# Talking-heads attention and Fourier mixing: score copies placed right behind the scores in five steps of a batch

## The chip, the core and the metric

The kernel runs on one core of a Trainium2 chip. The metric is the device time of one execution in microseconds (us), lower is better; the number compared is the median over runs. The engines of the core that matter here: TensorE (PE) does matmuls and transposes into PSUM, VectorE (DVE) and ScalarE (ACT) read PSUM and write SBUF, GpSimd (POOL) works on SBUF alone and starts many of the transfers, SyncE (SP) starts the others.

## The reference

Two blocks, in float32, for 8 batches of 448 positions and 12 heads of 64:

```python
scores = scale * np.matmul(q, k.transpose(0, 1, 3, 2))
scores = np.einsum('bhij,hg->bgij', scores, w_pre)        # heads are mixed
attn = np.exp(scores - np.max(scores, axis=-1, keepdims=True))
attn = attn / (np.sum(attn, axis=-1, keepdims=True) + 1e-09)
attn = np.einsum('bhij,hg->bgij', attn, w_post)           # and mixed again
attn_out = np.matmul(attn, v)
# x: (8, 448, 768), the heads side by side
mixed = np.real(np.fft.fft(np.fft.fft(x, axis=1), axis=2))
u = x + mixed
un = (u - mean(u)) / sqrt(var(u) + 1e-06)
out = u + np.maximum(un @ w_ch1, 0.0) @ w_ch2             # 768 -> 3072 -> 768
```

## The kernel before

The program has two stages. The mixing stage (`mix_phase`) makes u, the feed-forward stage (`ffn_phase`) makes the output. Only the mixing stage is touched.

**How the mixing stage is tiled.** The rows of a batch are cut into 8 blocks, and the blocks into 23 steps (`GS`); 8 batches make 184 steps (`TOT`). A step handles 10 positions with all 12 heads: two tiles of 5 positions, x = 0 and 1. Below, s is the number of a step and m = s mod 23 its place in the batch.

**What happens to a step T**, in the order of its data:

- *Scores* (`emit_qk`, matmuls at L628): q times k for a block and a pair of heads, into two PSUM tiles called "ms". Two copies on ACT (`copy`, L489) bring them to SBUF as "Sb". A block needs three such calls.
- *Gather* (`emit_gather`, L645): four transfers that SP starts turn rows of Sb into "Kr", where the heads of one position lie on partitions. Issued five steps ahead.
- *First head mix* (`emit_premix`, L656), two steps ahead: PE writes "mx", two PSUM tiles, one for each x, one buffer each.
- *Maximum* (`emit_max`, L663, DVE) of each mx, negated, as "nmx".
- *Exponential* (`emit_exp`, L670, ACT) of each mx with nmx as bias, into "PP", with the row sum into "den"; reading the sum out is an instruction of its own behind each.
- *Scaling* (`emit_scale`): DVE adds a constant to the sums (L677) and takes the reciprocal (L678), POOL multiplies PP (L680).
- *Second head mix* (`emit_postmix`, L690), in the step itself: PE writes "po". DVE transposes it into "Pv" (`emit_turn`, L703).
- *Values* (`emit_av`, L720): Pv times v for a group of two blocks, into two "ms" tiles; copies on ACT into "XT".

Beside these run "full" jobs: transposes of the next batch's q and k (`emit_xpose`, L601, copied half by ACT and half by DVE, all at L489), transposes of XT (`emit_x`, L764), and the Fourier products (`emit_z`, L829; `emit_s2`, L845, whose results DVE adds into X at L856 and L858). Each takes one or two "ms" tiles. DVE also does one conversion of the feed-forward weights in each step ("conv", `wts.deal(1)`, lines 250 to 310), for the double-precision inputs.

**The four "ms" buffers.** The pool `pms` has 4 buffers in turn. A job's matmuls are emitted at once; the copy that empties its tiles is put into the list `pend` and emitted by `flush()`. A fifth tile waits on the copy out of the first. `take` empties the list before each "full" job, and `room(2)` before scores and values when it would hold more than four.

**What sets the order.** The stage runs under `manual_schedule`: PE, DVE, ACT and POOL execute in the order in which the loop emits. One step is emitted in one of two orders, for even and for odd s:

```python
ORDERS = tuple(o.split() for o in (
    "pre post flush AV max0 exp0 "
    "QK max1 exp1 turn scale conv full gather",
    "pre post flush max0 max1 QK exp0 "
    "AV turn exp1 scale conv gather full flush"))
```

"pre", "max", "exp" and "scale" are of step s + 2, "post" and "turn" of step s, "gather" of step s + 5. The words "QK", "AV" and "full" take those jobs whose due time has come. A batch begins at an even s or an odd one in turn, so a given m has the even order in half of the batches and the odd order in the others.

**The five places.** In m = 0, 2, 5, 13 and 15 two more jobs that use "ms" tiles follow the scores, or take their place beside a second set of scores. m = 0: scores, L845, L764. m = 2: two scores, L845. m = 5 and 13: scores, L764, L601. m = 15: scores, L601 twice. In the first, second and last batch some of these jobs are missing: steps 23, 166 and 174 have one of the two, step 25 has two scores alone, step 176 has no scores.

Of the kernel before, what the change touches and what calls it, by code (L numbers as in the profile page):

```python
# [45 lines left out]
GS = BLOCK_AT[-1]  # L46
# [47 lines left out]
AT_QK = ((0, 2, 1), (0, 1, 2), (0, 1, 2), (1, 2, 2),  # L94
         (0, 1, 2), (0, 1, 2), (0, 1, 2), (0, 1, 2))
AT_AV = ((1, 2, 4), (0, 1, 3), (1, 3, 5), (1, 3, 4))
AT_X = ((13, 0), (23, 1), (28, 3), (29, 2))
AT_Z = (39, 40, 40, 42)
AT_S = ((42, 44), (46, 48))
# [351 lines left out]
def mix_phase(ctx, tc, rest, ident, q, k, v, w_pre, w_post, u_scr, u_rev, wts, lead):  # L451
# [39 lines left out]
    def flush():  # L491
        while pend:
            pend.pop(0)[1]()

    def room(n):
        if sum(e[0] for e in pend) + n > 4:
            flush()
# [138 lines left out]
    def emit_gather(T):  # L636

        Kr = pkr.tile([P, 2, S], F32, name="Kr", tag="Kr")
        n, j = at_step[T]
        Sb, rs = blocks[n]["Sb"], blocks[n]["rs"]  # L640
        row = _row(Sb)
        for z in range(2):
            for x in range(2):
                p0 = 64 - R * rs + 4 * j + 2 * z + x
                (nc.gpsimd if x and T < 3 else nc.sync).dma_start(  # L645
                    out=Kr[64 * x:64 * x + KR, z, :],
                    in_=_ap(Sb, p0 * row, [[rs * row, 2 * R], [S, 6], [1, S]]))
        steps[T]["Kr"] = Kr
# [25 lines left out]
    def emit_scale(T):  # L674
        PP, den = steps[T]["PP"], steps[T]["den"]
        rcp = psm.tile([P, 2], F32, name="rcp", tag="rcp")
        nc.vector.tensor_reduce(rcp[:, :], den[:, :, :], axis=AX.X, op=ALU.add)  # L677
        nc.vector.reciprocal(out=rcp[:, :], in_=rcp[:, :])  # L678
        for x in range(2):
            nc.gpsimd.tensor_scalar(PP[:, x, :], PP[:, x, :], rcp[:, x:x + 1], 1.0,  # L680
                                    op0=ALU.mult, op1=ALU.mult)
# [203 lines left out]
    def due(kind, at, fn):  # L885
        fill[kind].append((at, len(fill[kind]), fn))
# [4 lines left out]
    for b in range(B):  # L891
# [31 lines left out]
        for n in range(NG):  # L923
            for pr in range(3):
                due("AV", f + GROUP_AT[n + 1] + AT_AV[n][pr],
                    lambda a=b * NG + n, pr=pr: (emit_av(a, pr), None))
            at, gi = AT_X[n]
            if b == B - 1 and n > 1:
# [27 lines left out]
    def take(kind, s):  # L956
        large = 0
        while fill[kind] and fill[kind][0][0] <= s:
            fn = fill[kind].pop(0)[2]
            if kind == "none":  # L960
                large += bool(fn())
            elif kind == "full":
                flush()
                pend.extend((1, e, None) for e in fn())
            else:
                room(2)
                evs, n = fn()
                pend.extend((1, e, n) for e in evs)
        return large

    s = int(min(v_[0][0] for v_ in fill.values()))
    ET = mybir.EngineType
    with tc.manual_schedule(engines={ET.PE, ET.DVE, ET.Activation, ET.Pool}):
        while s <= TOT - GS + AT_X[-1][0]:
            old = len(later)
            n = take("none", s)
            ahead, now = 0 <= s + LM < TOT, 0 <= s < TOT
            for op in ORDERS[s % 2]:
                if op == "flush":
                    flush()  # L980
                elif op in fill:
                    take(op, s)
                elif op == "conv":
                    if s >= 4:
                        wts.deal(1)
                elif op == "gather":
                    if 0 <= s + LG < TOT:
                        if any(e[2] is not None and e[2] <= at_step[s + LG][0] for e in pend):
                            flush()
                        emit_gather(s + LG)  # L990
                elif op == "scale":
                    if ahead:
                        emit_scale(s + LM)
                    for _ in range(old if s < TOT + 5 else 0):
                        later.pop(0)()

                    if s < TOT - 3:
                        for _ in range(min(len(folds), 1 if n and s > 3 else 2)):
                            folds.pop(0)()
                elif op in ("post", "turn"):  # L1000
                    if now:
                        (emit_postmix if op == "post" else emit_turn)(s)
                elif ahead:
                    (emit_premix if op == "pre" else emit_max if op[0] == "m"
                     else emit_exp)(s + LM, *map(int, op[3:]))
            s += 1
        flush()
        wts.deal(1000)
# [484 lines left out]
@with_exitstack  # L1493
def kernel(
    ctx: ExitStack,
    tc: tile.TileContext,
    q: bass.AP,
    k: bass.AP,
    v: bass.AP,
    w_pre: bass.AP,  # L1500
    w_post: bass.AP,
    moe_w_ch1: bass.AP,
    moe_w_ch2: bass.AP,
    out: bass.AP,
):
    nc = tc.nc
    base = ctx.enter_context(tc.tile_pool(name="base", bufs=1))
    scr = ctx.enter_context(
        tc.tile_pool(name="scr", bufs=1, space=bass.MemoryType.DRAM))
    ident = base.tile([P, P], F32, name="ident")  # L1510
    make_identity(nc, ident[:, :])
    u_scr = [scr.tile([S + 1, DM], F32, name=f"u_{b}") for b in range(B)]
    u_rev = [scr.tile([S + 1, DM], F32, name=f"v_{b}") for b in range(B)]
    ub_scr = [scr.tile([7, P, NK, TB // 2], F32, name=f"ub_{t}") for t in range(NTB)]
    wts = _Weights(nc, moe_w_ch1, moe_w_ch2, scr)
    lead = _Lead(ctx, tc, ident, u_scr, u_rev)
    rest = ExitStack()
    fold_rest, parts = mix_phase(tc, rest, ident, q, k, v, w_pre, w_post, u_scr, u_rev,
                                 wts, lead)
    ffn_phase(tc, rest, ident, u_scr, u_rev, wts, ub_scr,  # L1520
              out.rearrange("b s d -> (b s) d"), fold_rest, parts,
              lead)
# [31 lines left out]
```

## Time and profile before

| quantity | value |
|---|---|
| median of 3 runs | 2296.27 us (2294.4 to 2301.48) |
| profiled execution | 2299.42 us, of which the span from the first to the last instruction is 2297.6 us |
| granted TensorE clock, mean | 0.998 |
| mixing stage, steps 0 to 181 | 36.5 to 776.2 us of the span |
| PE busy in the stretch from 100 to 215 us | 112.7 of 115.0 us |
| one score copy (L489, Sb) | 0.54 us, 378 of them on ACT |
| one exponential (L670) | 0.63 us, 368 |
| one maximum (L663) | 0.62 us, 368 |
| one scaling (L680) | 0.65 us, 368 |

Durations and waits are taken from one profiled execution, by the hardware profiler. In its lines, an engine's name is followed by the line of the program, the operation, and out<-in by the program's names of tiles. In a timeline the first two numbers are the start, in us from the beginning of the span, and the duration; "x16" merges 16 instructions that follow each other; "[0.23 <-ACT Sb L489]" says that the engine was idle for 0.23 us before and that a copy on ACT ended this. A line of the table of waits gives the total, how often, and the longest. A matmul's end is modelled, so a PE that is shown busy can still be slowed down. Where two exponentials are shown with their read-outs (ACTIVATION_READ_ACCUMULATOR), the end of the pair is the end of the second read-out.

### The profile page before, as it was taken

The numbers are of one execution on the slowest core, as the hardware profiler recorded it, in microseconds if no ns is written. First come the engines' busy times: TensorE is split into PE (matmuls) and PEld (weight loads), VectorE is DVE, ScalarE is ACT, GpSimd is POOL, SyncE is SP. The second block draws the span as 40 slices with busy tenths as digits, with TensorE's granted clock in tenths as the row PEclk, the third lists the DMA queues.
The fourth block names the chain that finished last, engine by engine and source line by source line (L and its number), as shares of the span: only waits on it lengthen the run. The fifth ranks groups of instructions, "written<-read, shape, count | busy, mean of one in ns | idle before, by whom it ended". The sixth has DMA issues, their size and how long they took to land.

```text
span 2297.6 us, 60793 instructions
## 1 busy us (share of the span) xinstructions
PE 2249.2 (98%) x22894; PEld 1740.7 (76%) x22894; DVE 1711.2 (74%) x3640; ACT 1167.1 (51%) x3330; POOL 1292.1 (56%) x1805
## 2 busy tenths in 40 slices
PE   7999999999999999999999999999999999999998
PEld 3455555555554677777899999999999899999998
DVE  5778787888877757776877787778778777765545
ACT  4676767767676533231445445444444445434434
POOL 7677878879768541221555555546555645454334
PEclk9999999999999999999999999999999999999999
DMA  7566565666756475649677887788787987795664
GB/s 185 168 178 181 168 192 171 190 179 181 202 151 190 143 265 182 230 162 327 191 181 180 252 214 184 212 195 242 204 197 184 277 188 174 191 257 121 143 146 76
DMA packets 228063, 439.45 MB, mean 191 GB/s; under 512 B 35964, under 2 KB 149558, under 8 KB 227772
## 3 DMA queue, kind: packets, MB, share of 16 engines
q1 hardware_dynamic: 156620, 301.52, 38.2%
q0 software_dynamic: 68864, 133.00, 30.4%
q8 instruction: 183, 3.00, 0.6%
q10 hardware_dynamic: 2288, 1.05, 0.2%
q14 instruction: 108, 0.88, 0.1%
HBM read 213.16 MB, written 143.16 MB: 155 GB/s over the span
## 4 chain that ended last, share of the span: by engine, by line
PE 87%; DVE 5%; DMA 3%; ACT 2%; issue 1%; POOL 1%; SPq 1%; ACTq 0%; DVEq 0%; POOLq 0%
PE psP L1213 18%; PE psP L1335 14%; PE psR L1213 9%; PE psR L1335 7%; PE mx L656 6%; PE ms L720 6%; PE ms L628 5%; PE po L690 5%; PE psQ L1213 4%; PE psQ L1335 3%; PE psP L1290 3%; PE ms L845 2%; PE ms L601 2%; DMA Kr<-Sb 1%; PE psR L1290 1%
## 5 line engine op out<-in xcount | busy, mean ns | idle before, releaser
L1369 POOL DMA_DIRECT2D out_dram<-od x172 | 209.1, 1276 | 261.7 <-DVE od L1357 175.3
L680 POOL TENSOR_SCALAR PP<-PP,rcp 128x448 f32<-128x448 f32 x368 | 234.6, 647 | 170.2 <-DVE rcp L678 123.8
L670 ACT ACTIVATE PP<-mx,nmx 128x448 f32<-128x448 f32 x368 | 230.2, 631 | 165.2 <-DVE nmx L663 157.2
L663 DVE TENSOR_REDUCE nmx<-mx 128x1 f32<-128x448 f32 x368 | 212.5, 618 | 101.2 <-PE mx L656 99.1
L1176 POOL TENSOR_TENSOR hq<-h 128x128 f32<-128x128 f32 (+1 forms) x210 | 130.0, 619 | 255.9 <-ACT h L1235 122.3
L1363 ACT COPY od<-psP 128x192 f32<-128x192 f32 x488 | 156.1, 320 | 172.0 <-PE psP L1335 170.6
L1366 DVE TENSOR_TENSOR od<-od 128x768 f32<-128x768 f32 x210 | 201.3, 972 | 52.7 <-ACT od L1363 52.3
L703 DVE STREAM_TRANSPOSE Pv<-po 128x896 f32<-128x896 f32 x184 | 203.7, 1107 | 2.9 <-PE po L690 2.1
L489 ACT COPY Sb<-ms 124x448 f32<-124x448 f32 (+1 forms) x378 | 181.7, 540 | 46.0 <-PE ms L628 19.2
L656 PE MATMUL mx<-Kr,kw 60*32 60x448 f32 x2944 | 192.2, 549 | 4.3 <-ACT PP L670 2.3
L628 PE MATMUL ms<-kT,qT 64*32 64x448 f32 (+1 forms) x3072 | 191.6, 545 | 3.9 <-ACT qT L489 2.8
L720 PEld LDWEIGHTS ms<-Pv,vv 64*64 64x64 f32 x5376 | 138.1, 132 | 73.7 <-issue 48.8
L690 PE MATMUL po<-PP,kw 60*32 60x448 f32 x2944 | 184.0, 537 | 1.2 <-POOL PP L680 1.1
L1213 PE MATMUL psP<-qs,w1t 128*128 128x256 f32 x744 | 179.2, 380 | 2.4 <-DVE h L1234 1.5
L1213 PE MATMUL psP<-ks,w1t 128*128 128x256 f32 x744 | 179.3, 380 | 0.4 <-DVE h L1234 0.3
L720 PE MATMUL ms<-Pv,vv 64*64 64x120 f32 (+1 forms) x5376 | 160.8, 263 | 3.6 <-ACT Sb L489 2.2
L254 POOL TENSOR_SCALAR wst<-wst 128x256 f32<-128x256 f32 (+1 forms) x76 | 118.6, 1569 | 67.2 <-ACT wst L265 66.9
L1213 PEld LDWEIGHTS psP<-qs,w1t 128*128 128x128 f32 x744 | 139.5, 190 | 19.4 <-DVE h L1234 1.9
L1213 PEld LDWEIGHTS psP<-ks,w1t 128*128 128x128 f32 x744 | 139.5, 190 | 17.2 <-DVE h L1234 0.7
L1213 PE MATMUL psP<-ub,w1t 128*128 128x256 f32 x528 | 127.2, 379 | 1.1 <-DVE h L1234 1.1
L1234 DVE TENSOR_TENSOR h<-h,psP 128x512 f32<-128x512 f32 x42 | 28.8, 686 | 127.9 <-PE psP L1213 112.3
L1335 PE MATMUL psP<-w2t,hq 128*128 128x192 f32 x490 | 122.5, 332 | 1.2 <-DVE od L1357 1.2
(199 smaller groups left out, 5301.6 us busy)
## 6 DMA issues: line engine op xcount, KB each, us to landing
Kr<-Sb SPq DMA_DIRECT2D x730, 105.0 KB
out_dram<-od POOLq DMA_DIRECT2D x172, 384.0 KB, 6.3
qs<-ub SPq DMA_DIRECT2D x89, 384.0 KB
ks<-ub SPq DMA_DIRECT2D x88, 384.0 KB
ub<-ub SPq DMA_DIRECT2D x79, 384.0 KB
w1t<-w SPq DMA_DIRECT2D x42, 384.0 KB
w2t<-w SPq DMA_DIRECT2D x42, 384.0 KB
raw<-in_moe_w_ch_dram SPq DMA_DIRECT2D x32, 384.0 KB
```

The costliest lines, as they stand in the source:

```text
L628: nc.tensor.matmul(pss[x][o:o + hi - lo, :S], st["qT", xx][64 * x:64 * x + 64, y, lo:hi], st["kT", xx][64 * x:64 * x + 64, y, :], start=Tr ...
L656: nc.tensor.matmul(mx[x][64 * z + o:64 * z + o + 32, :S], kw1[64 * x:64 * x + KR, o:o + 32], Kr[64 * x:64 * x + KR, z, :], start=True, sto ...
L663: nc.vector.tensor_reduce(nmx[:, :], steps[T]["mx"][x][:, :S], axis=AX.X, op=ALU.max, negate=True)
L670: nc.scalar.activation(steps[T]["PP"][:, x, :], steps[T]["mx"][x][:, :S], ACTF.Exp, bias=steps[T]["nmx", x][:, :], accum_out=steps[T]["den ...
L680: nc.gpsimd.tensor_scalar(PP[:, x, :], PP[:, x, :], rcp[:, x:x + 1], 1.0, op0=ALU.mult, op1=ALU.mult)
L690: nc.tensor.matmul(po[o:o + 32, z, :S], kw2[64 * z:64 * z + KR, y, :], PP[64 * z:64 * z + KR, :, c * HS:(c + 1) * HS], start=True, stop=True)
L703: nc.vector.transpose(turned[a]["Pv"][:, j, :].rearrange("p (z s) -> p z s", z=2), steps[T]["po"][:, :, :S])
L720: nc.tensor.matmul(pss[y][64 * x:64 * x + 64, :nu * R], st["v", pr][64 * y:64 * y + 64, x, jb * D:(jb + 1) * D], _ap(Pv, 64 * y * rp + 32 ...
L1213: mm = nc.tensor.matmul(p[:, m, :], w1[i][:, kc, m * P:(m + 1) * P], ub[:, kc, :], start=i in (0, 4, 1)[:3 - seed] and m == kc == 0, stop= ...
L1335: nc.tensor.matmul(ps[j, key][:, :DQ], a, b, start=m in (0, 4), stop=True, skip_group_check=True)
L1366: eng.tensor_tensor(D[j][:, :, :], D[j][:, :, :], D[k][:, :, :], op=ALU.add)
L1369: nc.gpsimd.dma_start(out=acc[t, r, d], in_=D[j][:, :, :], accum_op=ALU.add)
```

## The change

After the word "QK" of a step whose m is in `TWO`, all that stands in `pend` is emitted at once. In a step of the even order the score copies thus come on ACT behind the first exponential and in front of the second; in a step of the odd order they come in front of both. Before, they came behind both, when the next "full" job was taken or at the next "flush". In the other 18 places of a batch nothing changes.

```diff
 AT_AV = ((1, 2, 4), (0, 1, 3), (1, 3, 5), (1, 3, 4))
+TWO = (0, 2, 5, 13, 15)
 AT_X = ((13, 0), (23, 1), (28, 3), (29, 2))
...
                 elif op in fill:
                     take(op, s)
+                    if op == "QK" and s >= 0 and s % GS in TWO:
+                        flush()
                 elif op == "conv":
```

The function that it calls, unchanged:

```python
    def flush():
        while pend:
            pend.pop(0)[1]()
```

## The prediction

> **What bounds the kernel now.** I read the page's first part, then the table of waits, then the timeline engine by engine around the five steps that the change names.
>
> ```profile
> PE 2249.2 (98%) x22894; PEld 1740.7 (76%) x22894; DVE 1711.2 (74%) x3640; ACT 1167.1 (51%) x3330; POOL 1292.1 (56%) x1805
> ```
>
> TensorE (PE) has almost no gap, so the end moves by what PE waits. The waits that the change aims at are those for a copy of scores (Sb, L489), in microseconds, times, longest:
>
> ```profile
> PE ms L601 <- ACT Sb L489: 6.9, 19, 1.2
> PE ms L845 <- ACT Sb L489: 2.7, 6, 0.6
> ```
>
> Together 9.6 us: that is the most there is to gain. Below, m is the step's place in its batch, a step starts at its first L656 matmul, and bare times run from that start. Step 97 (m = 5, odd) on PE:
>
> ```profile
> 434.79 0.96 PE L628 MATMUL ms<-kT,qT 64*32 64x448 f32 x16
> 435.68 0.91 PE L764 MATMUL ms<-ident,XT 128*113 128x128 f32 x6
> 436.82 0.98 PE L601 MATMUL ms<-ident,rawq 128*128 128x128 f32 x7 [0.23 <-ACT Sb L489]
> 437.73 0.98 PE L656 MATMUL mx<-Kr,kw 60*32 60x448 f32 x16
> ...
> 440.99 0.61 PE L656 MATMUL mx<-Kr,kw 60*32 60x448 f32 x8
> ```
>
> L628 (scores) and L764 take the four "ms" buffers; L601 needs the first one back and waits 0.23 us for its copy. Next step at 437.73, the one after at 440.99. ScalarE (ACT) in it:
>
> ```profile
> 435.00 0.63 ACT L670 ACTIVATE PP<-mx,nmx 128x448 f32<-128x448 f32 x1 [0.46 <-DVE nmx L663]
> ...
> 436.14 0.20 ACT L670 ACTIVATION_READ_ACCUMULATOR PP<-mx,nmx 128x1 f32 x1
> 436.24 0.96 ACT L489 COPY Sb<-ms 124x448 f32<-124x448 f32 x2
> ...
> 440.71 0.20 ACT L670 ACTIVATION_READ_ACCUMULATOR PP<-mx,nmx 128x1 f32 x1
> ```
>
> The exponentials run from 435.00 to 436.34, the copies behind them. The next pair ends at 440.91, 0.08 us before the step at 440.99 opens: its L656 overwrites the "mx" buffers that they read. VectorE (DVE):
>
> ```profile
> 436.45 0.16 DVE L677 TENSOR_REDUCE rcp<-den 128x2 f32<-128x4 f32 x1
> 436.64 0.17 DVE L678 RECIPROCAL rcp<-rcp 128x2 f32<-128x2 f32 x1
> 436.72 1.29 DVE L310 TENSOR_TENSOR wst<-wst 128x256 f32<-128x256 f32 x1
> 437.94 1.12 DVE L489 COPY qT<-ms 128x512 f32<-128x512 f32 x1
> 438.89 1.11 DVE L663 TENSOR_REDUCE nmx<-mx 128x1 f32<-128x448 f32 x2
> ```
>
> The sum (L677) needs both exponentials, and behind it DVE is packed up to the next maxima (L663), which the next exponentials need. In step 59, where ACT was late by chance, DVE stood still there:
>
> ```profile
> 276.60 0.16 DVE L677 TENSOR_REDUCE rcp<-den 128x2 f32<-128x4 f32 x1 [0.92 <-ACT PP L670]
> ```
>
> What late exponentials cost PE, step 18 (m = 18) shows:
>
> ```profile
> 103.78 1.20 PE L656 MATMUL mx<-Kr,kw 60*32 60x448 f32 x12
> ...
> 108.43 0.96 PE L656 MATMUL mx<-Kr,kw 60*32 60x448 f32 x16
> ```
>
> Its first half opened when the first exponential was done, 0.56 us before the second one ended at 104.34. The step lasts 4.65 us; the other batches' m = 18 last 4.04 to 4.07. No gap is recorded, yet the lateness of the second exponential is paid in full. So a step opens, in effect, at the end of the previous step's second exponential + 0.06.
>
> **What the Trainium skill says.** "PSUM — Partial Sum Buffer", section "Engine vs sequencer instructions": the queues of ScalarE, VectorE and GpSimd are strict first in, first out, and matmuls keep program order; step 59's line agrees (0.92 us of standing still). "TensorEngine Tiling (Array Packing)", section "PSUM Bottleneck": tiling speeds up the matmuls, not the emptying of PSUM; agreed: 16 score matmuls hold PE 0.89 us in the excerpt (434.79 to 435.68), the two copies ACT 0.96. "Trainium Kernel Development and Optimization", section "Performance Expectations": matmul busy time is a bad metric; agreed by step 18, so I compare the lengths of steps.
>
> **The change part by part.** Nothing is added or removed. On PE the order of instructions is the same row for row, likewise on DVE and POOL. On ACT the score copies of m = 0, 2, 5, 13, 15 move: in even steps in front of the second exponential, in odd steps in front of both. SP's gathers shift by one or two places against a store: nothing, since PE waits 0.8 us in all for Kr in this stage. Prices from the timeline: a pair of copies 0.96 us, starting 0.10 us after the scores end; a pair of exponentials 1.34, one 0.72; the waiting product can start 0.58 after the first copy's start; L677 0.10 after the last exponential. Each follower overlaps by 0.12.
>
> *Odd step (97).* Scores end at 2.46. Copies 2.56 to 3.52 instead of 2.95 to 3.91, so L601 starts at about 3.25 instead of 3.53: +0.28 of gain. The exponentials move from 1.72-3.06 to 3.40-4.74. The next step could open at 4.17 but opens at 4.80, where it opened at 4.45: loss 0.35. Then DVE: L677 at 4.84 instead of 3.17. With c for the weight instruction (1.29 here), the maxima come at 4.84 + c + 1.14 = 7.27 instead of 5.61; the exponentials end 2.05 later, and the step after next opens at 9.38 instead of 7.71: loss 1.67.
>
> *Even step (82, m = 13).* First exponential as before, copies 2.59 to 3.55, second exponential to 4.15 (was 3.08). Next step at 4.21 instead of 4.47: gain 0.26. L677 is 1.06 later; the maxima with c = 0.28 at 5.87 instead of 5.50, the exponentials at 7.92: inside the step's 3.83 (4.21 + 3.83 = 8.04). Gain 0.26 stays.
>
> The same working for all, loss at the start of the second step after, in us:
>
> - m = 5. Odd 51, 97, 143: 1.5, 1.7, 1.5. Even 28, 74, 120: the maxima at 4.25 + c + 1.14, c 0.8 to 1.04; loss 0.56 each. 166 has no third product, and its next step moves from 3.26 to 4.21: 0.95. Sum 7.3.
> - m = 13. Odd 13, 151, 105: 0.35, 0.35, 0.26; 59, where PE had waited 1.0, gains 0.4. Even 82, 128 gain 0.26 each; 36 loses 0.25, 174 (no third product) 0.95. Sum 1.3.
> - m = 15. DVE copies two chunks (1.6 us), and the next scores need the buffer of the first. Odd 15, 61, 107, 153: 1.05, 0.6, 0.8, 0.55. Even 38, 84, 130: 0.3, 0.2, 0.15. Sum 3.6.
> - m = 0. No PE wait to remove. DVE's four L856/L858 (1.95) come behind L677 and free a buffer that the next step's first product needs: odd 69, 115, 161 end them at 7.4, where that product stood at 6.2: 1.2 each; even 92, 138: 6.9 against 6.1, 0.8 each; 46 nothing, PE was late itself. 23: next step 3.85 to 5.4: 1.6. Sum 6.8.
> - m = 2, four copies. Odd 71, 117, 163: exponentials end at 5.60, L677 at 5.70, L856/L858 to 8.4, maxima 8.3 instead of 7.3: 1.1 each. 25 has no third product, next step 3.01 to 5.66: 2.65. Even 48, 94, 140: second exponential to 4.98, 0.64 each. Sum 7.8.
> - Steps 0, 2, 5: PE waits there for transfers as well; bounds -1 and +4, I take 1.5.
>
> POOL's scaling (L680) comes 1.1 to 1.7 later behind L678; median 3.3 us lie between its end and its reader L690, so I take nothing. What is queued behind it on POOL (loads, folds) has steps of room; where POOL is behind (a slack of 0.05 at steps 35, 36, 53, 104, 167, 168) the bounds are -2 (PE's lateness hides its wait) and +3.
>
> Sum: 7.3 + 1.3 + 3.6 + 6.8 + 7.8 + 1.5 = 28.3. Other waits of PE in this stage (L720 2.2, L656 on ACT 2.3, L628 1.1, POOL 1.1, "issue" 1.1, Kr 0.8: 8.6 us) partly vanish under a later PE; I take off a third, 3. Left: +25. The profiled execution took 2299.4 (span 2297.6 + 1.8), so 2324; against the median of the runs, 2296.3, it is 2321.
>
> **Rivals.**
>
> 1. Only the first delay counts: DVE makes good its lateness. Odd 0.35 x 11 + 0.27 x 3 + 0.4 x 3, 23 and 25 4.2, 166 and 174 1.9, minus eight even gains of 0.26: about +10, 2306. For it: DVE is 74% busy overall. Against: in step 97 it has no idle from L663 to the next L663.
> 2. Gains and losses cancel: 2296, if m = 0 and 2 cost nothing and m = 5 half. Against: steps 25, 166, 174 can only lose.
> 3. Faster: buffers come back early and the exponentials' delay is covered. All 9.6 us go: 2287. It decides if L656 can open without the end of both exponentials, or if DVE's work behind L677 has over 1.7 us of room. For it: the waits are there, and step 6's L656 stood 1.4 us behind the exponentials in 97. Against: step 18, and the 0.08 us at 440.99.
>
> That the copies stay where they were is ruled out by ACT's order.
>
> **How the numbers follow.** My forecast 0.66, rival 1 0.16, rival 2 0.08, rival 3 0.10. Under about 0.3% (6.9 us) this measurement can't be told from no change. Faster 0.10, same 0.08, slower 0.82. Forecast's own bounds: 28.3 + 2.5 + 3 = 34 above, 28.3 - 2.5 - 2 - 8.6 = 15 below; down to rival 1 at +10: 2305 to 2330.
>
> **What would show it.** Right: L677 waits for ACT PP in odd steps by about 1.7 us, PE mx L656 <- ACT PP and ms waits for DVE grow, the waits for Sb shrink under 4 us; steps 97 and 98 together last 9.4 us, not 7.7; step 25 lasts 5.7, not 3.0. FFN stage unchanged. Wrong: if step pairs keep their length, or the page's DVE idle does not move to L677.

## The result

The median went from 2296.74 to 2325.63 us, six executions of each on the same chip (2293.8 to 2303.92 and 2320.33 to 2328.85). The medians lie 28.9 us apart; the ratio is 1.0118, 95% interval 1.0105 to 1.013, which is 27.1 us of the time before. The profiled execution took 2326.35 us with a span of 2324.0, at a mean granted clock of 0.996 (before: 0.998).

The mixing stage, steps 0 to 181, took 768.3 us instead of 739.7: 28.6 more. What comes behind it took 1519.1 instead of 1521.4, and that figure lies between 1517.7 and 1521.0 in the other kernels below, so no change of the FFN stage shows. From here on, line numbers are one higher than before (L656 is L657 and so on) because of the new line at the top, and three higher below the loop.

The first part of the page of the kernel after (busy time of each engine, share of the span, instructions):

```profile
PE 2274.3 (98%) x22894; PEld 1758.0 (76%) x22894; DVE 1702.1 (73%) x3640; ACT 1167.5 (50%) x3330; POOL 1291.5 (56%) x1805
```

The same 22894 matmuls are busy for 25.1 us longer, while the idle time of PE grew by 1.3 us only (span minus busy: 48.4 before, 49.7 after). Who looks for the loss among the gaps of PE does not find it. Part 5 of the page (group of instructions | busy us, mean ns of one | idle before it, with what ended it) shows where it lies. Before:

```profile
L656 PE MATMUL mx<-Kr,kw 60*32 60x448 f32 x2944 | 192.2, 549 | 4.3 <-ACT PP L670 2.3
```

And after:

```profile
L657 PE MATMUL mx<-Kr,kw 60*32 60x448 f32 x2944 | 219.3, 551 | 14.7 <-ACT PP L671 9.1
```

One matmul is as long as before (549 and 551 ns), but the group covers 27.1 us more: its sixteen instructions are torn apart, since part of them wait for the second exponential while the others run. The table of waits of the kernel after, PE (us in total, times, longest):

```profile
PE mx L657 <- ACT PP L671: 9.1, 11, 1.9
...
PE ms L629 <- DVE kT L490: 3.9, 7, 0.8
...
PE ms L602 <- ACT Sb L490: 0.5, 1, 0.5
```

The waits for score copies are gone as intended (6.9 to 0.5 at L602, 2.7 to none at L846). And DVE:

```profile
DVE nmx L664 <- PE mx L657: 88.7, 89, 6.0
...
DVE rcp L678 <- ACT PP L671: 73.9, 44, 3.5
```

The sum (L678) now stands still for 73.9 us in all, where the table of before has 14.6 in 16 waits. Here is step 97 again, which starts at 448.84 (start, us, instruction). PE:

```profile
450.35 0.96 PE L629 MATMUL ms<-kT,qT 64*32 64x448 f32 x16
...
451.98 0.98 PE L602 MATMUL ms<-ident,rawq 128*128 128x128 f32 x7
453.04 1.20 PE L657 MATMUL mx<-Kr,kw 60*32 60x448 f32 x12
...
454.06 0.56 PE L657 MATMUL mx<-Kr,kw 60*32 60x448 f32 x4
...
457.11 1.20 PE L657 MATMUL mx<-Kr,kw 60*32 60x448 f32 x12
```

L602 no longer waits. The next step opens in two halves. The line with x12 merges two groups: by the starts of the single matmuls, the eight of L657 for the first tile start from 453.04 on, and the first four for the second tile at 453.66, 0.06 us after the end of the second exponential; the line at 454.06 is the other four of that tile. In the kernel before all sixteen start within 0.44 us. ACT:

```profile
451.40 0.97 ACT L490 COPY Sb<-ms 124x448 f32<-124x448 f32 x2 [1.29 <-PE ms L629]
452.25 0.65 ACT L671 ACTIVATE PP<-mx,nmx 128x448 f32<-128x448 f32 x1
...
456.33 0.63 ACT L671 ACTIVATE PP<-mx,nmx 128x448 f32<-128x448 f32 x1 [1.18 <-DVE nmx L664]
```

ACT stands idle for 1.29 us because it waits for scores; behind that wait two exponentials are queued whose inputs, the maxima, are both there at 451.00, before the scores are. DVE:

```profile
453.71 0.16 DVE L678 TENSOR_REDUCE rcp<-den 128x2 f32<-128x4 f32 x1 [1.69 <-ACT PP L671]
...
453.99 0.78 DVE L311 TENSOR_TENSOR wst<-wst 128x256 f32<-128x256 f32 x1
454.69 1.13 DVE L490 COPY qT<-ms 128x512 f32<-128x512 f32 x1
455.60 1.16 DVE L664 TENSOR_REDUCE nmx<-mx 128x1 f32<-128x448 f32 x2
```

The sum waits 1.69 us; the conversion, the qT copy and the maxima follow it without a gap; and the exponentials of the next step start at 456.33, so late that the step after next is late too.

The growth of the mixing stage by place, counted from each of the five places up to the next one, so that a delay that shows one or two steps later is with its cause (steps 0, 2, 5 apart; differences of two profiled executions, worked out from the starts of the steps):

| place | predicted, us | measured, us | in odd steps | in even steps |
|---|---|---|---|---|
| m = 0 | 6.8 | 3.1 | 23: 1.57; 69, 115, 161: 0.41, 0.26, 0.35 | 46, 92, 138: 0.42, 0.10, 0.01 |
| m = 2 | 7.8 | 11.4 | 25: 4.17; 71, 117, 163: 1.84, 1.57, 1.74 | 48, 94, 140: 0.57, 0.66, 0.85 |
| m = 5 | 7.3 | 2.5 | 51, 97, 143: 0.49, 2.29, 0.91 | 28, 74, 120: 0.10, -0.05, 0.33; 166: -1.61 |
| m = 13 | 1.3 | 1.1 | 13, 59, 105, 151: 0.34, -0.60, 1.41, 0.44 | 36, 82, 128: -0.91, -0.27, -0.27; 174: 0.95 |
| m = 15 | 3.6 | 7.0 | 15, 61, 107, 153: 1.34, 1.22, 1.55, 1.28 | 38, 84, 130, 176: 0.69, -0.14, 0.89, 0.15 |
| steps 0, 2, 5 | 1.5 | 3.5 | 5: -1.04 | 0: 3.02; 2: 1.53 |
| sum | 28.3 | 28.6 | 21.5 | 7.0 |

The sum agrees, its terms do not. Two of the figures are not the place's own, -1.61 at step 166 and a part of 3.02 at step 0; the section on why the prediction was right takes them up. The experiments ask whether the mechanism is right all the same, and which terms were wrong.

### The profile page after: what moved, and what is told of

Read it like the earlier page. It is cut to its first block, busy times and chain, and to the rows that moved or that the text cites. A ratio compares the mean times of both kernels' runs of the same rounds, so it can differ in the third digit from the quotient of the medians.

```text
span 2324.0 us, 60841 instructions
## 1 busy us (share of the span) xinstructions
PE 2274.3 (98%) x22894; PEld 1758.0 (76%) x22894; DVE 1702.1 (73%) x3640; ACT 1167.5 (50%) x3330; POOL 1291.5 (56%) x1805
## 4 chain that ended last, share of the span: by engine, by line
PE 87%; DVE 4%; issue 4%; ACT 2%; POOL 1%; DMA 1%; SPq 0%; DVEq 0%; POOLq 0%; ACTq 0%
PE psP L1216 17%; PE psP L1338 14%; PE psR L1216 9%; PE mx L657 7%; PE psR L1338 7%; PE ms L629 6%; PE ms L721 6%; PE po L691 5%; PE psQ L1216 4%; PE psQ L1338 3%; PE psP L1293 2%; PE ms L846 2%; PE ms L830 1%; ACT PP L671 1%; DMA Kr<-Sb 1%
## 5 line engine op out<-in xcount | busy, mean ns | idle before, releaser
L657 PE MATMUL mx<-Kr,kw 60*32 60x448 f32 x2944 | 219.3, 551 | 14.7 <-ACT PP L671 9.1
L629 PE MATMUL ms<-kT,qT 64*32 64x448 f32 (+1 forms) x3072 | 204.5, 544 | 9.6 <-DVE kT L490 3.9
L691 PE MATMUL po<-PP,kw 60*32 60x448 f32 x2944 | 206.9, 539 | 0.7 <-issue 0.6
L629 PEld LDWEIGHTS ms<-kT,qT 64*32 64x32 f32 (+2 forms) x3072 | 63.9, 105 | 81.6 <-issue 54.7
```

The lines of the kernel that those rows point to most:

```text
L629: nc.tensor.matmul(pss[x][o:o + hi - lo, :S], st["qT", xx][64 * x:64 * x + 64, y, lo:hi], st["kT", xx][64 * x:64 * x + 64, y, :], start=Tr ...
L657: nc.tensor.matmul(mx[x][64 * z + o:64 * z + o + 32, :S], kw1[64 * x:64 * x + KR, o:o + 32], Kr[64 * x:64 * x + KR, z, :], start=True, sto ...
L691: nc.tensor.matmul(po[o:o + 32, z, :S], kw2[64 * z:64 * z + KR, y, :], PP[64 * z:64 * z + KR, :, c * HS:(c + 1) * HS], start=True, stop=True)
```

## The experiments

Where not said otherwise a kernel is the one after with the edit shown. The theory: the late exponentials hold PE by two ways, the first gate (the next step's L657 needs both exponentials done) and the queue of DVE (L678 waits for them, and the next maxima stand behind it).

**1 and 2. Odd steps alone, even steps alone.**

```diff
-                    if op == "QK" and s >= 0 and s % GS in TWO:
+                    if op == "QK" and s >= 0 and s % 2 and s % GS in TWO:
```

> The copies move only in the steps of the odd order, where they pass both exponentials. My theory (late exponentials hold the next first head mix, and the sums behind them hold the vector engine): the step lengths of the changed kernel put 21.6 us on the odd steps, so about 2318 us. Rival (the first wait alone, both orders alike): half of the loss, about 2311.

Measured: 2315.81 against 2297.03 before, ratio 1.0076 [1.0059, 1.0093]. The second kernel has `s % 2 == 0` in place of `s % 2`:

> The copies move only in the steps of the even order, where they pass one exponential. My theory: the step lengths put 7.0 us on the even steps, so about 2304 us, 5 of it in the first batch and m = 2. Rival (both orders alike): about 2311.

Measured: 2310.64, ratio 1.0056 [1.0039, 1.0072]. The odd steps came out 2 us below what was expected. The even ones missed: 6.6 us above the expectation, at the figure of the rival. The two shares add up to 1.32%, where the whole change measured 1.18%; the intervals cover that. A part of the miss is found: in the profile of the even steps the mixing stage is 10.7 us longer, 3.7 more than the 7.0 of the table, and all of these 3.7 lie at steps 166 to 168 (+2.07 here, -1.61 in the kernel after), where step 168 waits for transfers of Kr (8.33 us here, 6.71 before, 4.64 in the kernel after). The rest, some 3 us between this profile and the medians, stays open. What stands: both parities lose, and odd steps more than even ones (2313.9 to 2317.2 us against 2308.7 to 2312.2).

**3 and 4. The queue of DVE taken out.** In the five places the sum and the scaling are emitted at the end of the step, behind DVE's other work of that step, and the copies stay early. On POOL the scaling thereby comes behind the other work of the step, too.

```diff
                 elif op == "scale":
-                    if ahead:
+                    if ahead and not (s >= 0 and s % GS in TWO):
                         emit_scale(s + LM)
...
+            if ahead and s >= 0 and s % GS in TWO:
+                flush()
+                emit_scale(s + LM)
             s += 1
```

> The changed kernel, but in the five steps the sums, reciprocals and scaling of the exponentials are emitted at the end of the step, behind the weight conversion and the copies of the full jobs. My theory: the vector engine no longer stands still, its wait for ACT PP (73.9 us) falls under 40, and what is left is the first wait of the next head mix, the steps 25, 166 and 174 and the first batch: about 2311 us. Rival (the time goes to the first wait alone, or to transfers): stays at 2325.

And the control, the same move in the kernel before, with the copies late as they were there:

> Control: the kernel before with the same later place of sums and scaling in the five steps and the copies where they were. My theory: no engine waits for the sums there, so 2297 within 3 us. If it moves by more, the run sums_late has to be read against this one.

Measured: 2317.7, ratio 1.0083 [1.0066, 1.0099], about halfway between the theory (2311) and the rival (2325); the control 2304.52, ratio 1.0031 [1.0019, 1.0043]. The control was expected at no change and missed: the move itself costs some 7 us, mostly two steps behind m = 2 (steps 50, 96 and 142 are 1.1 us longer each), and the waits of L691 for POOL's scaling become 5.2 us in all (1.1 before). The move did what it was for; the table of waits of the third kernel, DVE:

```profile
DVE rcp L678 <- ACT PP L671: 13.5, 11, 3.8
```

From 73.9 back to 13.5. Step by step, m = 2 in 71, 117, 163 falls to 0.54, 0.67, 0.64 (from 1.6 to 1.8), and m = 15 in 61, 107, 153 to 0.39, 0.57, 0.38 (from 1.2 to 1.6), while step 13, where only the first gate was predicted to act, keeps its 0.34. Steps 25 and 38 lose more than in the kernel after (5.64 and 3.86 us); there the granted clock was 0.50 for 6.8 and 3.4 us in this profile. Taken as it stands, the loss falls from 1.18% to 0.83%. If the move costs the same with and without early copies, the early copies cost 0.52% when the queue of DVE is out, and 1.18% when it is in. Each end has an interval of some 0.15%. That the costs add is not shown, and single steps speak against it: the control loses 1.75, 0.90 and 0.98 us at m = 2 in 71, 117, 163 by the move alone, more than the move and the early copies together. By these two readings the queue of DVE holds a third to a little over half of the loss; its exact share stays open.

**5. Only the first copy early, in the kernel before.** It asks whether there is something to gain if the second exponential is delayed by one copy instead of two.

```diff
+ONE = (2, 13)
...
                      else emit_exp)(s + LM, *map(int, op[3:]))
+                if op == ("QK", "exp0")[s % 2] and 2 * GS < s < TOT - 10 and s % GS in ONE and pend:
+                    pend.pop(0)[1]()
             s += 1
```

> A version that should beat both: only the first score copy is moved, between the two exponentials, in m = 2 and 13 of the batches 2 to 7. It frees the buffer that the next product waits for and makes one exponential 0.6 us late instead of two 1.7 us. My theory: the wait of 0.2 to 0.6 us goes and nothing behind it is late: 0.3 us in each of ten steps and 0.5 us in the odd ones of m = 2, about 2293 us (-4), at the edge of what can be told. Rival (any move in front of an exponential costs more than it frees): 2300 or more.

Measured: 2298.97 against 2297.48, ratio 1.0003 [0.9993, 1.0013]: no gain, between the theory (2293) and the rival (2300). m = 2 gained as expected (-0.39, -0.70, -0.37, -0.15, -0.38 and 0.03 us in 48 to 163), but m = 13 lost 0.23, 0.23 and 0.68 us in 82, 128 and 151, and 1.34 in 105, a step that lasts 4.45 to 5.58 us in kernels that move nothing in it. The timeline of PE in its step 82, which starts at 368.36, says why:

```profile
371.53 0.66 PE L602 MATMUL ms<-ident,rawq 128*128 128x128 f32 x4
372.58 0.55 PE L602 MATMUL ms<-ident,rawq 128*128 128x128 f32 x3 [0.39 <-ACT Sb L490]
```

The seven transposes of L602 need both score buffers: four go into the first, the other three wait for the second copy, which now stands behind the second exponential. The next step opens at 4.70 instead of 4.47.

**6. Without the places that have no third product**, that is from step 26 on and without 166 and 174.

```diff
-                    if op == "QK" and s >= 0 and s % GS in TWO:
+                    if op == "QK" and s > 25 and s not in (166, 174) and s % GS in TWO:
```

> The changed kernel without the steps of the first batch and without 23, 25, 166 and 174, where a third product is missing and nothing waits for the copies. My theory: the step lengths put about 10 us there (3.0, 1.5, -1.0 in the first batch, 1.6 at 23, 4.2 at 25, the rest at 166 and 174), so about 2315 us. Rival (those steps only shift a wait that is there anyway): stays at 2324.

Measured: 2315.65, ratio 1.0083 [1.0068, 1.0099], as the theory expected. The places left out hold 10.3 us in the table above (3.5 for steps 0, 2, 5; 0.34, 1.34, 1.57, 4.17, -1.61, 0.95 for 13, 15, 23, 25, 166, 174), and the growth of the median falls from 28.9 to 18.2. The term of 166 does not belong in this sum: with 166 left as it was, the stretch behind it is again 1.59 us shorter than before.

**7 and 8. One place alone**, to size the terms for m = 2 and m = 0.

```diff
-TWO = (0, 2, 5, 13, 15)
+TWO = (2,)
```

> The copies move in m = 2 alone. My theory with m = 0 as the source of a part of what m = 2 shows: the odd steps 71, 117 and 163 cost 1.1 us each and not the 1.6 to 1.8 of the changed kernel, the even ones 0.6 each, step 25 2.6 to 4.2, step 2 1.5: 9 to 11 us, about 2306. Rival (m = 2 stands alone): 1.6 to 1.8 each again, 13 us, 2309.

With `TWO = (0,)`:

> The copies move in m = 0 alone. As I predicted it (the next step's first product waits for the buffer that L856/L858 free): odd 69, 115, 161 cost 1.2 us each, even 0.8. By the changed kernel's profile instead: 0.3 each in the step itself, and 0.5 more shows in m = 2; with 3.0 at step 0 and 1.6 at step 23 about 6 to 7 us, 2303.

Measured: 2305.44, ratio 1.0032 [1.002, 1.0045], near the 2306 of the theory; and 2306.5, ratio 1.0043 [1.0028, 1.0057]. Alone, m = 2 costs 0.88, 1.07, 1.12 us in 71, 117, 163, 0.52 to 0.59 in even steps and 4.07 in 25. Alone, m = 0 costs 0.13, 0.25, 0.36 in 69, 115, 161, and then another 0.35, 0.25, 0.19 in the m = 2 steps behind them, though nothing was moved there; 1.57 in 23 and 3.74 in step 0. Its total is 3.5 us above the expectation; 2.5 us of that lie at steps 143 to 145, far from any m = 0, which I put down to chance; no run tests that.

**9. Places that the change leaves alone**, as a test of the theory on steps where it had not been fitted.

```diff
-TWO = (0, 2, 5, 13, 15)
+TWO = (9, 11, 17, 19)
...
-                    if op == "QK" and s >= 0 and s % GS in TWO:
+                    if op == "QK" and s > GS and s % GS in TWO:
```

> The same early copies at four other places, m = 9, 11, 17 and 19 of the batches 1 to 7, where PE waits for no buffer in the kernel before. My theory prices it from step lengths alone: the next step can't open before 4.80 us in odd steps and 4.21 in even ones, against lengths of 3.3 (m = 9), 3.8 (11), 4.14 (17) and 4.65 (19): 1.5, 1.0, 0.66, 0.15 in odd, 0.9, 0.4, 0.07, 0 in even steps, 15.5 us in all, and up to 5 more from the vector engine's queue: 2313 to 2318. Rival (the loss belongs to the five places and their third product): 2300 or less.

Measured: 2318.87, ratio 1.0082 [1.0064, 1.01], which is 18.8 us (21.8 by the medians) against 15.5 to 20.5. The size is the theory's, and most single steps too: m = 9 odd 0.94 + 0.52 us (two steps), m = 17 odd 0.10 + 0.59, m = 17 even 0.06 to 0.12, as expected. m = 9 even lost 0.9 to 2.3 instead of 0.9. The clear miss is m = 11 even, 1.9 us instead of 0.4: in these even steps the products with the values stand in front of the scores, so the copies start 4.12 us after the start of the step, 1.5 later than in step 82, and the second exponential stands behind them.

**10. Both copies early, but the second one on DVE**, in m = 13; everything else as in experiment 5.

```diff
+    def split():
+        return 2 * GS < s < TOT - 10 and s % GS == 13
...
-        engs = ENG["QK"] if n > 1 else "ad"
+        engs = ENG["QK"] if n > 1 and not split() else "ad"
...
+                if op == "turn" and split() and pend:
+                    pend.pop(0)[1]()
```

> As first_copy, but in m = 13 the second score copy goes to DVE, behind its transpose, since L601 there needs both buffers. My theory: m = 2 gives 0.15 to 0.7 us in each of five steps as in the profile of first_copy (2.0 in all), m = 13 gives 0.2 in each of five instead of costing 0.2: 3 us together, 2294. Rival (the vector engine has no room for another 0.63 us copy): m = 13 longer than before, 2297 or more.

Measured: 2291.1 against 2297.05 (21 and 25 executions), ratio 0.9984 [0.9975, 0.9992]: 3.7 us faster by the ratio and 6.0 by the medians, faster than both kernels of the case. Its step 82 starts at 366.28. PE:

```profile
369.45 1.14 PE L602 MATMUL ms<-ident,rawq 128*128 128x128 f32 x7
370.52 0.98 PE L660 MATMUL mx<-Kr,kw 60*32 60x448 f32 x16
```

ACT:

```profile
368.87 0.53 ACT L490 COPY Sb<-ms 124x448 f32<-124x448 f32 x1
369.29 0.64 ACT L674 ACTIVATE PP<-mx,nmx 128x448 f32<-128x448 f32 x1
```

DVE:

```profile
369.40 0.58 DVE L490 COPY Sb<-ms 124x448 f32<-124x448 f32 x1
370.13 0.16 DVE L681 TENSOR_REDUCE rcp<-den 128x2 f32<-128x4 f32 x1
```

The seven transposes run together, the second exponential is delayed by one copy only, and the copy on DVE fits in front of the sum, which had to wait there. All sixteen L660 of the next step run together from 4.24 on. m = 13 gains 0.52, 0.24, 0.53, 0.23, 0.23 us in 59 to 151, m = 2 gains 0.18 to 0.65.

## Why the prediction was right, and where its terms were not

**The mechanism** is shown. Early copies push the exponentials back; this costs time at the next step's first product and, through DVE's order, at the step after. The queue of DVE: 73.9 us of waits at L678, which experiment 3 takes back to 13.5 and with it a third to a half of the loss. The gate: what stays then, at steps such as 13, the group L657 that is torn apart, and experiment 9, whose loss was worked out from this gate for steps in which nothing had been moved before. A direct test of the gate, a second pair of "mx" buffers, was not made. Step 97 went as worked out: copies 2.56 to 3.53 after its start (predicted 2.56 to 3.52), exponentials to 4.76 (4.74), the second half of the next step at 4.82 (4.80), the sum at 4.87 (4.84). So did step 25, PE:

```profile
140.01 1.71 PE L629 MATMUL ms<-kT,qT 64*32 64x448 f32 x32
143.57 1.20 PE L657 MATMUL mx<-Kr,kw 60*32 60x448 f32 x12 [1.85 <-ACT PP L671]
```

It started at 138.51; eight of the next step's L657 open at 5.06, the other eight from 5.68 on, so in effect the step opens at 5.68 (predicted 5.66, before 3.01).

One thing that the prediction takes from the Trainium skill ("PSUM — Partial Sum Buffer", section "Engine vs sequencer instructions"), that matmuls keep program order, does not hold to the letter for the starts in this trace: in step 97 four of L691 start at 453.82, 0.24 us before the last four of L657, which the loop emits in front of them. The mechanism does not need it.

**Rival 1** (DVE makes good its lateness, 2306) falls with the result (2325.6), with experiment 3 and with the odd steps of m = 2 and 15: both lose more with the queue than without. **Rival 2** (they cancel) falls with the result; experiment 6 shows that the places that can only lose are not the whole loss. **Rival 3** (2287) named as its deciding point that L656 opens without the end of both exponentials: it opens for eight of sixteen at the end of the first exponential, but the other eight hold the step. That 9.6 us of waits were there to take was right, and nearly all of them went; their worth was not, since a wait of PE for a copy is shorter than the delay that its removal brings.

**What failed is the sizing of three terms, and the allowance.** They hid each other: m = 5 is 4.8 us below its figure and m = 0 3.7, m = 2 is 3.6 above and m = 15 3.4. That their sum came so near is luck.

*m = 5: "With c for the weight instruction (1.29 here)".* I took c from its old place. It took 0.78 at the new one, and 0.41 instead of 1.03 in step 74; over the six steps other than 166 it was 2.5 us shorter in all, so the maxima came earlier. The reason, as far as the two ends below show it, is what POOL does beside it. The timeline of POOL, before:

```profile
436.71 1.02 POOL L790 TENSOR_TENSOR xs<-xs 113x383 f32<-113x383 f32 x1
```

After:

```profile
453.35 1.14 POOL L800 TENSOR_TENSOR xq<-xs 113x191 f32<-113x191 f32 x2
```

Before, c started at 436.72, in the same moment as L790, and ended 0.28 us behind it. After, it started inside L800 and ended 0.28 behind that one. The Trainium skill, "SBUF — State Buffer", section "Who interferes with whom", says that VectorE and GpSimd share one pair of ports as an exclusive lock; both ends agree with it, and it would have told me not to carry c over. With c as it was, the working for step 97 closes: the step after next opens its second half 8.88 us after the start of step 97 instead of 7.71, a loss of 1.17, and the predicted 1.67 less 0.51 is 1.16. The other 1.1 of the 2.29 up to the next place lie in step 104, which lasts 3.8 to 5.4 us in the profiled kernels.

Over half of the 4.8 is not c but 166, put at +0.95 and measured at -1.61. That is not its own: in experiments 6 and 7, which leave 166 alone, the same stretch is 1.59 and 1.60 shorter than before. It falls on step 168 (last section), so this term is not measured.

*m = 0: "DVE's four L856/L858 (1.95) come behind L677 and free a buffer that the next step's first product needs".* It does not need it. In step 116, behind m = 0 in 115, PE of the kernel after:

```profile
533.88 1.70 PE L721 MATMUL ms<-Pv,vv 64*64 64x120 f32 x56
```

And DVE:

```profile
534.22 0.55 DVE L859 TENSOR_TENSOR X<-X,ms 113x383 f32<-113x383 f32 x1
```

The product starts 0.89 us before the last of the four has ended at 534.77, and it writes both of its tiles from the first matmuls on; so it was given other buffers, and the four are not handed out strictly in turn, as the section on the kernel before has it. The lateness shows at m = 2 instead: alone, m = 2 costs 0.88 to 1.12 (1.1 predicted), and m = 0 alone leaves 0.19 to 0.35 there; together they cost 1.57 to 1.84, more than the two added. That DVE carries it on is my reading: counted from the start of step 115, DVE's maxima for the step after start at 7.26 us in the kernel after and at 5.85 in the kernel before.

*m = 2* has a second surplus, 1.5 us at step 25 (4.17 instead of 2.65), which no term of the prediction covers. It lies in step 26, which lasts 6.27 us instead of 4.16, chiefly because its matmuls themselves run longer. Before:

```profile
135.41 1.05 PE L690 MATMUL po<-PP,kw 60*32 60x448 f32 x16
```

And after:

```profile
144.72 2.14 PE L691 MATMUL po<-PP,kw 60*32 60x448 f32 x12
```

From 144.8 to 148.2 us the granted clock was 0.50, and a single L691 takes up to 0.95 us instead of 0.54. That follows PE's 1.85 us of waiting, its longest from step 0 to step 181 in this profile. In experiment 7 the same wait was followed by the same 3.4 us (4.07 us lost at step 25). In experiment 1 it was not: the wait was 1.86, the clock stayed at 1.00, and step 25 cost 2.57, nearly the predicted 2.65. So the surplus goes with the lower clock, not with the early copies alone; what decides whether the clock falls stays open.

*m = 15: "the next scores need the buffer of the first".* They need the second chunk itself, as data: it is the transposed k that they multiply with, and DVE copies it last. In step 131, behind m = 15 in 130, PE:

```profile
597.61 0.98 PE L629 MATMUL ms<-kT,qT 64*32 64x448 f32 x16 [0.72 <-DVE kT L490]
```

And DVE:

```profile
596.89 0.57 DVE L490 COPY kT<-ms 128x384 f32<-128x384 f32 x1
```

L629 starts 0.15 after that copy's end. A wait for data, one copy later than the buffer I had looked at: 7.0 instead of 3.6.

*Steps 0, 2 and 5* cost 3.5 instead of 1.5, near my upper bound: step 0 loses 3.0 (3.7 in experiment 8) in spite of its waits for transfers. A part of that is the clock's. Ahead of step 0 the granted clock falls to 0.50, for 6.8 us in the kernel before and for 10.2 in all others. In the kernel before this ended 0.2 us ahead of step 0; in the others it reaches 1.4 to 4.1 us into it (2.4 in the kernel after). With half of that time taken off, the four kernels that move step 0 (the one after and experiments 2, 3 and 8) all lose 1.8 us there, and the seven that leave it alone between -0.2 and 0.1. So I estimate 1.2 of the 3.0 us as the clock's and 1.8 as the copies'.

*"I take off a third, 3"* has no counterpart: idle of PE did not fall, and the sum before that allowance, 28.3, lies nearer to what was measured.

Of the signs that I named, L678 by 1.7 us in an odd step (1.69), PE's waits for ACT PP (2.3 to 9.1) and for DVE (kT, none to 3.9), Sb under 4 (0.5 at L602), step 25 and the FFN stage hold. Steps 97 and 98 lasted 8.27 us to the start of the first half and 8.88 to that of the second, where I had named 9.4 and before 7.71: less, because c was shorter.

## What to carry to other kernels

Before moving work to remove a wait, ask what stands behind it in its engine's queue: here 9.6 us of waits for a copy were all but removed, and the exponentials behind the copies made the kernel 28.9 us slower. Compare the lengths of steps, not the idle time of the full engine: 25.1 of 26.4 us of this loss are recorded as busy time. Where a buffer is wanted early and something urgent shares the engine, one copy can go to an engine that waits at that moment: in m = 13 that turned the loss of experiment 5 into a gain, while in m = 2 moving one copy on ACT alone was enough.

## What the runs showed that I had not expected

An instruction of DVE took 0.49 us or 2.07 for the same form, depending on when POOL started beside it. In the control of experiment 4, DVE in step 50:

```profile
240.50 2.07 DVE L251 TENSOR_SCALAR tmp<-raw 128x256 uint32<-128x256 uint32 x1
```

And POOL:

```profile
240.39 1.96 POOL L786 TENSOR_TENSOR xs<-X 113x384 f32<-113x384 f32 x2
```

It ended 0.22 us behind both of POOL's instructions; in the kernel before it started at 240.46, when POOL's pair was 0.34 us from its end, and took 0.49. So a move of 1.6 us by POOL or DVE can cost or save as much as the change itself does in a step.

Single steps swing with the transfers. Step 168 lasted 6.58 to 8.39 us in six of the twelve profiled kernels and 4.64 to 5.21 in the other six; where it was long, a copy of scores waited for Kr (3.66 us in the kernel before). In the four profiles where it lasted 8.06 us or more, PE's matmuls in it also ran at a granted clock of 0.50 for 3.4 us. It was short in all five kernels that move the copies of step 163, and long in six of the other seven, so it may not be chance alone; no run separates that. A place's figure from one profile can thus be off by 2 us and more, and the small terms of the table above are read with that in mind; the repeated pattern of the odd steps is not moved by it.
